# Two loads cut in two, and two value projections taken in turn, in a one-core attention-plus-MLP kernel

## The chip, the core and the metric

The kernel runs on one core of a Trainium2 chip. The core has a matrix engine (TensorE, PE in the profile, with its weight loads as PEld), a vector engine (VectorE, DVE), a scalar engine (ScalarE, ACT), a general one (GpSimd, POOL) and SyncE (SP), which here only issues transfers (DMAs). The metric is the device time of one execution in microseconds (us); lower is better. The time before is 173.61 us, the median of three runs (173.14, 173.61 and 174.13).

## The reference

```python
def reference(A_x, A_wqkv, A_w_phi, A_wo, B_x, B_w1, B_b1, B_w2):
    def _A_ref(x, wqkv, w_phi, wo):
        B, S, D = x.shape
        H = 32; Dh = D // H
        qkv = (lambda x, *d: x.transpose(*d))((x @ wqkv).reshape(B, S, 3, H, Dh), 2, 0, 3, 1, 4)
        q, k, v = qkv[0], qkv[1], qkv[2]
        pq = jnp.einsum("bhsd,hdf->bhsf", q, w_phi)
        pk = jnp.einsum("bhsd,hdf->bhsf", k, w_phi)
        phi_q = jnp.concatenate([_softmax(pq, axis=-1), _softmax(-pq, axis=-1)], axis=-1)
        phi_k = jnp.concatenate([_softmax(pk, axis=-1), _softmax(-pk, axis=-1)], axis=-1)
        kv = jnp.einsum("bhsf,bhsd->bhfd", phi_k, v)
        z  = jnp.einsum("bhsf->bhf", phi_k)
        num = jnp.einsum("bhqf,bhfd->bhqd", phi_q, kv)
        den = jnp.einsum("bhqf,bhf->bhq", phi_q, z)[..., None] + 1e-6
        o = num / den
        return (lambda x, *d: x.transpose(*d))(o, 0, 2, 1, 3).reshape(B, S, D) @ wo

    def _B_ref(x, w1, b1, w2):
        h = jnp.einsum("bsd,df->bsf", x, w1) + b1
        sp = jnp.log1p(jnp.exp(-jnp.abs(h))) + jnp.where(h > 0, h, jnp.zeros_like(h))
        act = h * jnp.tanh(sp)
        return jnp.einsum("bsf,fd->bsd", act, w2)

    x = A_x
    xn = _layernorm(x, axis=-1)
    return x + _A_ref(xn, A_wqkv, A_w_phi, A_wo) + _B_ref(xn, B_w1, B_b1, B_w2)
```

There are S = 2048 tokens of D = 512 numbers, 32 heads of 16 and F = 1792 hidden units, in bf16. A layer norm feeds two branches: an attention without a softmax over tokens (each head's 16 key or query features become 32 by two softmaxes) and a two-layer network with the Mish activation. Their sum is added to x.

## The kernel before

The tokens are cut into 16 tiles of 128 and four groups of four tiles. A tile of x is loaded with its tokens on the 128 partitions (`x_sb`), its mean and variance are taken on VectorE (line 165 and 167), it is normalised there (line 176) into `xn`, and it is turned so that the 512 features lie on the partitions in four blocks (`xnT`). For the first four tiles TensorE turns the tile by an identity (line 609) and VectorE or ScalarE copies the result (line 627); for the others a transposing DMA does it (line 181).

From `xnT` TensorE makes the keys' and queries' logits (`pl`, line 229, or 244 for the first two tiles), the values (`pv`, line 229) and the hidden units (`ph`, line 263). Each such product is a sum over the four feature blocks: four matmuls of 128x512 into one PSUM bank, with `xnT` as the weights for logits and values, and with the first-layer weights `w_sb` as the weights and four tiles of `xnT` streamed for hidden units. So a hidden unit needs all four tiles of a group, while values and logits need one tile. The values' weights are `wv`, four blocks of 128 rows by 512, in one tile of SBUF.

The order of all work is written out by hand in `STEPS`, a list of short names that are run one after the other; each engine takes its instructions in that order and waits on semaphores where data or a buffer isn't ready. The names that matter here, with the number of the tile, and after an `@` the PSUM bank:

- `LS t`: mean and variance of tile t, on VectorE. `RS t`: its inverse root, on ScalarE (`a`) or GpSimd (`p`). `AZ t`: the normalising, on VectorE.
- `TP t`: turning tile t on TensorE. `TC t`: the copy into `xnT`, by VectorE (`v`) or ScalarE (`a`).
- `F0`, `FD`: the keys' weights multiplied by w_phi, block by block, and their copies into `wkp`. The last of these copies on VectorE stands just ahead of `LS 2`.
- `LP i`: the logits of tiles 0 and 1, both tiles in turn for each feature block. `L 0 t`: the logits of tile t of group 0; `LC 0 t`: their copy.
- `V t`: the values of tile t. `VC t`: their copy, on ScalarE (`a`) or VectorE (`v`).
- `H u`: hidden unit block u, with 14 to a group; `H 6` is the first to run. `M u`: its activation on ScalarE.
- `LN`, `AP`: the norm of a later group; `WL`, `E`: logits and softmaxes.

In the stretch around the change the list reads: LP i; RS 2; LC 0 1; V 1; LS 3; AZ 2; RS 3; AZ 3; TP 2; V 0; TC 2; LC 0 0; TP 3; L 0 2; VC 1; TC 3; LC 0 2; H 6; L 0 3; VC 0.

The loads at the start are issued on SP, one behind the other in one queue: tile 0, tile 1, two blocks of the keys' weights, a transposing load of the rest (`wT`), tiles 2 and 3 together, `wv`, the first half of w1 (columns of hidden blocks 0 to 6), tiles 4 to 7, the rest of w1, tiles 8 to 11. ScalarE issues two small ones, the biases and w_phi (`wsrc`). The transfers of SP and ScalarE take eight semaphores in turn, and an issue first waits until the transfer eight before it has landed.

```python
    for t in range(2):
        nc.sync.dma_start(x_sb[:, t, :], x_v[:, t, :])
...
    nc.sync.dma_start(x_sb[:, 2:4, :], x_v[:, 2:4, :])
    nc.sync.dma_start(wv[:], wqkv_v[:, :, 2 * D : 3 * D])
    nc.sync.dma_start(w1_sb[:, :, 0 : 7 * P], w1_v[:, :, 0 : 7 * P])
    nc.sync.dma_start(x_sb[:, 4:8, :], x_v[:, 4:8, :])
```

Of the kernel before, what the change touches and what calls it, by code (L numbers as in the profile page):

```python
# [23 lines left out]
AW 256; AW 512; AW 128; AW 512; AW 256; AW 256; AW 512; AW 256; LS 0; AW 512; AW 512; LS 1; AW 256;  # L24
AW 256; AW 64; AW 128; RS 0 a; AW 512; PB @1; CB; AW 512; TW 0 @3; AZ 0; RS 1 a; AZ 1; TW 1 @0; TP 0
@2; TP 1 @5; TK 0 a; TC 0 a; WB v; TK 1 v; F0 0 @4; F0 1 @0; TC 1 v; F0 2 @2; FD 0 a; FD 2 a; FD 1
v; LS 2; F0 3 @1; FD 3 a; LP i @5,3; RS 2 a; LC 0 1 a; V 1 @1; LS 3; AZ 2; RS 3 p; AZ 3; TP 2 @0; V
0 @2; TC 2 v; LC 0 0 a; TP 3 @4; L 0 2 @5; VC 1 a; TC 3 a; LC 0 2 a; H 6 @4; L 0 3 @0; VC 0 v; LN 1;
LC 0 3 a; H 0 @1; H 1 @0; E 0 0; DX 2; AP 1 0; H 2 @5; AP 1 1; H 9 @2; M 2; H 3 @3; DX 3; M 1; M 9;
H 4 @5; M 0; M 6; H 10 @2; M 4; H 8 @1; KM; H 5 @5; H 11 @4; M 3; LN 2; M 8; E 0 1; M 5; H 7 @3; H  # L30
12 @5; M 10; AP 2 0; WL 1; M 11; H 17 @4; M 7; AM; L 1 0 @0; WL 2; L 1 3 @3; M 12; X 0 1; AP 2 1; X
# [31 lines left out]
def kernel(  # L63
# [12 lines left out]
    nc = tc.nc  # L76
    P = 128
    S, D, NH, DH, F = 2048, 512, 32, 16, 1792
# [3 lines left out]
    KT = D // P  # L82
# [4 lines left out]
    x_v = A_x.flatten_outer_dims().rearrange("(t p) d -> p t d", p=P)  # L87
    o_v = out.flatten_outer_dims().rearrange("(t p) d -> p t d", p=P)
    wqkv_v = A_wqkv.rearrange("(kt p) c -> p kt c", p=P)
# [17 lines left out]
    x_sb = persist.tile([P, NT, D], BF16, name="x_sb")  # L107
    xnT = persist.tile([P, NT, KT, P], BF16, name="xnT")
# [4 lines left out]
    wv = wts.tile([P, KT, D], BF16, name="wv")  # L113
# [27 lines left out]
    def bank(b, name, dtype=FP32):  # L141

        return ps.tile([P, 512], dtype, name=name, tag=f"bank{b}")
# [82 lines left out]
    def project(w, t, pp):  # L226

        for kt in range(KT):
            nc.tensor.matmul(  # L229
                pp, lhsT=xnT[:, t, kt, :], rhs=w(kt),  # L230
                start=(kt == 0), stop=(kt == KT - 1),
            )
        return pp

    pv_of, ph_of, pl_of = {}, {}, {}
# [12 lines left out]

    def value(t, b):
        pv_of[t] = project(values, t, bank(b, "pv")[:])  # L250

    def keep(t, copy):
        copy(
            vext[t // TPG % 2][:, t % TPG, :, 0:64],
            pv_of.pop(t).rearrange("p (j c) -> p j c", j=8),
        )
# [27 lines left out]
    def take(s, i, copy):  # L284
        if s not in p_of:
            p_of[s] = smx.tile([P, TPG, 512], BF16, name="p_sb")
        copy(p_of[s][:, i, :], pl_of.pop((s, i)))  # L287
# [238 lines left out]
    nc.scalar.dma_start(b1b[:], b1_v[:, :])  # L526
    with nc.allow_non_contiguous_dma(reason="tiny w_phi load"):
        nc.scalar.dma_start(wsrc[:], wphi_v)
    nc.sync.dma_start(x_sb[:, 2:4, :], x_v[:, 2:4, :])  # L529
    nc.sync.dma_start(wv[:], wqkv_v[:, :, 2 * D : 3 * D])  # L530
    nc.sync.dma_start(w1_sb[:, :, 0 : 7 * P], w1_v[:, :, 0 : 7 * P])
    nc.sync.dma_start(x_sb[:, 4:8, :], x_v[:, 4:8, :])
    nc.sync.dma_start(w1_sb[:, :, 7 * P : F], w1_v[:, :, 7 * P : F])
# [128 lines left out]
    def load_queries():  # L662
# [9 lines left out]
        "F0": lambda kt, b: fold(wT_of[0], kt, b), "FD": lambda kt, c: unfold(wkp, kt, copies[c]),  # L672
        "LN": stats, "AP": apply, "DX": load_tokens, "DW": load_weights, "WL": wide,
        "L": logits, "LC": lambda s, i, c: take(s, i, copies[c]),
        "V": value, "VC": lambda t, c: keep(t, copies[c]),
        "H": hidden, "M": mish,
        "E": extremes, "X": exponentials, "S": sums,
# [42 lines left out]
```

## Time and profile before

| | |
|---|---|
| median of three runs | 173.61 us |
| the profiled execution's own time | 174.09 us |
| its span in the profile | 172.3 us |
| TensorE busy | 168.1 us, 98% |
| VectorE busy | 141.8 us, 82% |
| ScalarE busy | 124.9 us, 72% |
| DMA engines' share, 8.6 to 12.9 us of the span | 9 tenths or more |
| granted TensorE clock | 0.999 |

Times in the trace count from the start of the span. A row of the timeline gives start, duration, engine, line, operation, and what is written from what; in brackets stands the engine's idle time before it and what ended it. A row of the chain gives start, duration and what the end of the run waited for. A row of a stretch gives its length, then for each engine its busy time and number of instructions (TensorE, weight loads, VectorE, ScalarE, GpSimd), the clock, the DMA engines' share and GB/s. A row of the DMA view gives the tile, the issuing engine, the number of issues, the size and the time from issue to landing. Matmuls overlap their neighbours, so four of them take less than the end of the last minus the start of the first.

### The profile page before, as it was taken

The numbers are of one execution on the slowest core, as the hardware profiler recorded it, in microseconds if no ns is written. First come the engines' busy times: TensorE is split into PE (matmuls) and PEld (weight loads), VectorE is DVE, ScalarE is ACT, GpSimd is POOL, SyncE is SP. The second block draws the span as 40 slices with busy tenths as digits, with TensorE's granted clock in tenths as the row PEclk, the third lists the DMA queues.
The fourth block names the chain that finished last, engine by engine and source line by source line (L and its number), as shares of the span: only waits on it lengthen the run. The fifth ranks groups of instructions, "written<-read, shape, count | busy, mean of one in ns | idle before, by whom it ended". The sixth has DMA issues, their size and how long they took to land.

```text
span 172.3 us, 2749 instructions
## 1 busy us (share of the span) xinstructions
PE 168.1 (98%) x1051; PEld 82.4 (48%) x1051; DVE 141.8 (82%) x220; ACT 124.9 (72%) x204; POOL 7.4 (4%) x21
## 2 busy tenths in 40 slices
PE   8989999999999999999999999999999999999993
PEld 3644444444444554454445644544444444554452
DVE  3677999989999999439989999799799998884333
ACT  3765989998999999789978989977282792432200
POOL 4021230200000000000000000000000000000000
PEclk9999999999999999999999999999999999999999
DMA  4997094276099200000000194309235628778641
GB/s 128 298 374 244 3 213 103 48 139 108 17 199 360 95 4 0 0 0 4 0 0 0 34 114 100 61 7 162 80 100 113 152 56 194 151 162 208 90 125 61
DMA packets 46297, 18.55 MB, mean 108 GB/s; under 512 B 38092, under 2 KB 46284, under 8 KB 46284
## 3 DMA queue, kind: packets, MB, share of 16 engines
q1 hardware_dynamic: 45584, 18.26, 44.7%
q10 hardware_dynamic: 700, 0.12, 0.4%
q8 instruction: 8, 0.13, 0.3%
q14 instruction: 5, 0.04, 0.1%
HBM read 7.10 MB, written 2.10 MB: 53 GB/s over the span
## 4 chain that ended last, share of the span: by engine, by line
PE 93%; DMA 3%; SPq 2%; issue 0%; DVE 0%
PE ph L263 28%; PE po L497 28%; PE pl L229 14%; PE pv L229 8%; PE po L504 8%; DMA wv<-in_A_wqkv_dram 3%; PE pnd L452 2%; PE pkv L421 2%; PE pwide L229 1%; SPq L523 1%; SPq L518 0%; SPq L529 0%; PE ptr L609 0%; SPq L522 0%; PE pfold L203 0%
## 5 line engine op out<-in xcount | busy, mean ns | idle before, releaser
L497 PE MATMUL po<-w_sb,acts 128*128 128x512 bf16 (+2 forms) x238 | 50.8, 366 | 0.0
L263 PE MATMUL ph<-xnT,w_sb 128*128 128x512 bf16 x224 | 50.3, 379 | 0.0
L274 ACT ACTIVATE acts<-ph,b1f 128x512 bf16<-128x512 f32 x56 | 35.8, 698 | 3.1 <-PE ph L263 3.0
L340 DVE TENSOR_REDUCE s<-e 128x128 f32<-128x2048 bf16 x16 | 36.3, 2276 | 0.5 <-ACT e L323 0.5
L263 PEld LDWEIGHTS <-w_sb 128*128 128x128 bf16 x224 | 21.6, 98 | 25.8 <-issue 0.2
L497 PEld LDWEIGHTS <-acts 128*128 128x128 bf16 x238 | 22.1, 98 | 23.6
L323 ACT ACTIVATE e<-e 128x2048 bf16<-128x2048 bf16 x16 | 30.4, 1915 | 0.0
L229 PEld LDWEIGHTS <-xnT 128*128 128x128 bf16 x184 | 17.5, 98 | 21.3 <-DMA wv<-in_A_wqkv_dram 1.1
L287 ACT CAST p_sb<-pl 128x512 bf16<-128x512 f32 x26 | 14.8, 589 | 4.8 <-PE pl L229 4.8
L511 DVE TENSOR_TENSOR x_sb<-po,x_sb 128x512 bf16<-128x512 f32 (+2 forms) x17 | 11.0, 657 | 8.3 <-PE po L504 8.3
L229 PE MATMUL pv<-wv,xnT 128*128 128x512 bf16 x64 | 15.4, 379 | 0.6 <-DMA wv<-in_A_wqkv_dram 0.6
L504 PE MATMUL po<-wqk,xnT 128*128 128x512 bf16 (+2 forms) x68 | 15.6, 366 | 0.0
L229 PE MATMUL pl<-wqk,xnT 128*128 128x512 bf16 x64 | 15.6, 379 | 0.0
L467 ACT COPY ds<-pnd 128x32 f32<-128x32 f32 x16 | 2.9, 183 | 16.5 <-PE pnd L452 16.5
L307 DVE TENSOR_TENSOR e<-p_sb,m 128x2048 bf16<-128x2048 bf16 x8 | 9.8, 1225 | 5.4 <-PE pkv L421 5.1
L165 DVE BATCH_NORM_STATS2 stats<-x_sb 128x6 f32<-128x512 bf16 x16 | 10.1, 680 | 4.6 <-DMA x_sb<-in_A_x_dram 4.6
L139 ACT ACT_TABLE_LOAD x10 | 12.8, 1283 | 0.2
L298 DVE TENSOR_TENSOR m<-m 128x512 bf16<-128x512 bf16 (+1 forms) x32 | 11.5, 359 | 1.1
L229 PE MATMUL pl<-wkp,xnT 128*128 128x512 bf16 x48 | 12.0, 379 | 0.0
L298 DVE TENSOR_TENSOR m<-p_sb 128x1024 bf16<-128x1024 bf16 x16 | 10.9, 682 | 0.5 <-ACT p_sb L287 0.5
L307 DVE TENSOR_TENSOR e<-m,p_sb 128x2048 bf16<-128x2048 bf16 x8 | 9.8, 1226 | 0.3
L374 DVE TENSOR_TENSOR e<-e,r 128x2048 bf16<-128x2048 bf16 x8 | 9.6, 1218 | 0.5 <-ACT r L349 0.5
(72 smaller groups left out, 130.3 us busy)
## 6 DMA issues: line engine op xcount, KB each, us to landing
w_sb<-in_B_w_dram SPq DMA_DIRECT2D x4, 896.0 KB, 8.4
out_dram<-x_sb SPq DMA_DIRECT2D x15, 128.0 KB, 2.0
x_sb<-in_A_x_dram SPq DMA_DIRECT2D x3, 512.0 KB, 8.6
wv<-in_A_wqkv_dram SPq DMA_DIRECT2D x1, 512.0 KB, 5.7
wqk<-in_A_wo_dram SPq DMA_DIRECT2D x1, 512.0 KB, 4.3
x_sb<-in_A_x_dram SPq DMA_DIRECT2D x2, 128.0 KB, 2.1
wkp<-in_A_wqkv_dram SPq DMA_DIRECT2D x1, 256.0 KB, 3.4
x_sb<-in_A_x_dram SPq DMA_DIRECT2D x1, 256.0 KB, 4.9
```

Source lines behind the costliest of these rows:

```text
L139: nc.scalar.preload_act_table_set(name)
L229: nc.tensor.matmul(pp, lhsT=xnT[:, t, kt, :], rhs=w(kt), start=(kt == 0), stop=(kt == KT - 1),)
L263: nc.tensor.matmul(ph_of[u][:], lhsT=w1_sb[:, kt, f * P : (f + 1) * P], rhs=xnT[:, g * TPG : (g + 1) * TPG, kt, :], start=(kt == 0), stop= ...
L274: nc.scalar.activation(acts[:, f, g * 512 : (g + 1) * 512], ph_of.pop(u)[:], ACT.Mish, bias=b1f[:, f : f + 1])
L287: copy(p_of[s][:, i, :], pl_of.pop((s, i)))
L298: nc.vector.tensor_tensor(out=m[:], in0=src[:, :, 0:half], in1=src[:, :, half : 2 * half], op=op)
L307: nc.vector.tensor_tensor(out=e_of[s][:].rearrange("p t j l c -> p (t j) l c")[:, :, pl, :].rearrange("p t (c e o) -> p t c e o", e=8, o=2 ...
L323: nc.scalar.activation(v, v, ACT.Exp)
L340: nc.vector.reduce_sum(t[:], pair(s, k).rearrange("p t j l (c e) -> p (t j l c) e", e=16), axis=AX.X)
L497: nc.tensor.matmul(po_of[t, c.stop][:, c], lhsT=acts[:, f, t * P : (t + 1) * P], rhs=w2_sb[:, f, c], start=(f == 0), stop=False,)
L504: nc.tensor.matmul(po_of[t, c.stop][:, c], lhsT=oT_of[t // 2][:, t % 2 * 4 + j, :], rhs=wo_sb[:, j, c], start=False, stop=(j == 3),)
L511: nc.vector.tensor_tensor(out=y, in0=po_of.pop((t, c.stop))[:, c], in1=y, op=ALU.add)
```

## The change

```diff
@@ STEPS @@
-v; LS 2; F0 3 @1; FD 3 a; LP i @5,3; RS 2 a; LC 0 1 a; V 1 @1; LS 3; AZ 2; RS 3 p; AZ 3; TP 2 @0; V
-0 @2; TC 2 v; LC 0 0 a; TP 3 @4; L 0 2 @5; VC 1 a; TC 3 a; LC 0 2 a; H 6 @4; L 0 3 @0; VC 0 v; LN 1;
+v; LS 2; F0 3 @1; FD 3 a; LP i @5,3; RS 2 a; LC 0 1 a; VA @1,2; LS 3; AZ 2; RS 3 p; AZ 3; TP 2 @0;
+VB; TC 2 v; LC 0 0 a; TP 3 @4; L 0 2 @5; VC 1 a; TC 3 a; LC 0 2 a; H 6 @4; L 0 3 @0; VC 0 v; LN 1;
@@ new function @@
+    def first_values(h, *b):
+
+        if h == 0:
+            for t, i in zip((1, 0), b):
+                pv_of[t] = bank(i, "pv")[:]
+        k = (2 * h, 2 * h + 1)
+        pairs = [(t, kt) for kt in k for t in (1, 0)] if h == 0 else [(t, kt) for t in (1, 0) for kt in k]
+        for t, kt in pairs:
+            nc.tensor.matmul(
+                pv_of[t], lhsT=xnT[:, t, kt, :], rhs=wv[:, kt, :],
+                start=(kt == 0), stop=(kt == KT - 1),
+            )
@@ loads @@
-    nc.sync.dma_start(x_sb[:, 2:4, :], x_v[:, 2:4, :])
-    nc.sync.dma_start(wv[:], wqkv_v[:, :, 2 * D : 3 * D])
+    for t in range(2, 4):
+        nc.sync.dma_start(x_sb[:, t, :], x_v[:, t, :])
+    for kt in (slice(0, 2), slice(2, 4)):
+        nc.sync.dma_start(wv[:, kt, :], wqkv_v[:, kt, 2 * D : 3 * D])
@@ names @@
+        "VA": lambda *b: first_values(0, *b), "VB": lambda: first_values(1),
```

Tiles 2 and 3 of x come by a transfer each, and `wv` by two transfers, of two row blocks each (half 0 and half 1). In place of V 1, TensorE runs VA: the first two feature blocks of the values of tiles 1 and 0, in turn, into two banks. In place of V 0 it runs VB: the other two blocks, first tile 1's, then tile 0's.

On TensorE, between the last matmul of LP and the turn of tile 3, the kernel before has these rows (`pv_230` is the bank of tile 1's values, `pv_246` that of tile 0's; `DMAHW7` is the semaphore of wv's transfer):

```order
L229 LDWEIGHTS xnT_86 [waits DMAHW7_49]
L229 MATMUL pv_230<-wv_91,xnT_86 128x512 [waits PE_49]
L229 LDWEIGHTS xnT_86
L229 MATMUL pv_230<-wv_91,xnT_86 128x512
...
L609 LDWEIGHTS xn_135 [waits DVE_49]
L609 MATMUL ptr_241<-ident_98,xn_135 128x128
...
L229 LDWEIGHTS xnT_86
L229 MATMUL pv_246<-wv_91,xnT_86 128x512
```

And the changed kernel has these at the same place (`pv_232` is tile 1's bank, `pv_233` tile 0's; `DMAHW0` and `DMAHW1` are the semaphores of the halves):

```order
L260 LDWEIGHTS xnT_86 [waits DMAHW0_49]
L260 MATMUL pv_232<-wv_91,xnT_86 128x512 [waits PE_49]
L260 LDWEIGHTS xnT_86
L260 MATMUL pv_233<-wv_91,xnT_86 128x512
...
L624 LDWEIGHTS xn_137 [waits DVE_49]
L624 MATMUL ptr_244<-ident_98,xn_137 128x128
...
L260 LDWEIGHTS xnT_86
L260 MATMUL pv_232<-wv_91,xnT_86 128x512 [waits DMAHW1_49]
```

The number and kind of TensorE's instructions are the same; the one wait for all of wv became a wait for each half, with the turn of tile 2 between them.

On SP the kernel before issues, after the transposing load of the keys' weights:

```order
L529 DMA x_sb<-in_A_x_dram 128x2x512
L530 DMA wv<-in_A_wqkv_dram 128x4x512
L531 DMA w_sb<-in_B_w_dram 128x4x896 [waits DMAHW0_49]
L532 DMA x_sb<-in_A_x_dram 128x4x512 [waits DMAHW1_49]
L533 DMA w_sb<-in_B_w_dram 128x4x896 [waits DMAHW2_49]
```

And the changed kernel:

```order
L543 DMA x_sb<-in_A_x_dram 128x512 x2
L545 DMA wv<-in_A_wqkv_dram 128x2x512 [waits DMAHW0_49]
L545 DMA wv<-in_A_wqkv_dram 128x2x512 [waits DMAHW1_49]
L546 DMA w_sb<-in_B_w_dram 128x4x896 [waits DMAHW2_49]
L547 DMA x_sb<-in_A_x_dram 128x4x512 [waits DMAHW3_49]
L548 DMA w_sb<-in_B_w_dram 128x4x896 [waits DMAHW4_49]
```

Every load behind the four stands two issues later in the queue, and each takes the semaphore two further on: the first half of w1 took that of the biases (`DMAHW0`) and takes that of w_phi (`DMAHW2`).

## The prediction

> **What bounds the kernel now.** I read the page first: its busy line and the head of its chain of waits.
>
> ```profile
> PE 168.1 (98%) x1051; PEld 82.4 (48%) x1051; DVE 141.8 (82%) x220; ACT 124.9 (72%) x204; POOL 7.4 (4%) x21
> PE 93%; DMA 3%; SPq 2%; issue 0%; DVE 0%
> ```
>
> TensorE is the kernel. The only thing beside it that weighs on the chain is one DMA. Next, the same chain in order of time:
>
> ```profile
> 4.19 5.69 DMA wv<-in_A_wqkv_dram
> 9.88 0.05 issue
> 9.93 1.04 PE pv L229 x4
> 10.96 0.22 PE ptr L609 x4
> 11.19 0.86 PE pv L229 x4
> ...
> 169.33 0.24 PE po L504 x4
> ```
>
> The values' weights land at 9.88 us and from 9.93 on TensorE runs without a break to 169.57. So only what makes the work after 9.93 start earlier, or opens a gap in it, can change the time. The views by stretch and by single matmuls give the size of the hole:
>
> ```profile
> 9.35:9.93 0.58, 0.01 (x1) 0.01 (x1) 0.58 (x2) 0.49 (x3) 0.00 (x0) 1.00 1.07 403
> 9.93:12.97 3.04, 3.04 (x20) 1.63 (x21) 1.94 (x6) 2.14 (x5) 0.88 (x2) 1.00 1.07 373
> 8.96 0.38 PE L244 MATMUL pl<-wkp,xnT 128*128 128x512 bf16 x1
> PE pv L229 <- DMA wv<-in_A_wqkv_dram: 0.6, 1, 0.6
> ```
>
> 0.58 us stand empty by the modelled ends. Four matmuls of this shape take 0.86 in the unbroken chain, 0.216 apart, so the one after 8.96 could have begun at 9.18: the most that can be won here is 9.93 - 9.18 = 0.75 us, 0.43% of the run.
>
> **What stands just behind the hole.** The timeline of the same stretch shows a second chain, of VectorE, that is nearly as late:
>
> ```profile
> 7.14 0.69 DVE L160 CAST wkp<-pfold 128x512 bf16<-128x512 f32 x1 [0.16 <-PE pfold L151]
> 8.46 0.69 DVE L165 BATCH_NORM_STATS2 stats<-x_sb 128x6 f32<-128x512 bf16 x1 [0.62 <-DMA x_sb<-in_A_x_dram]
> 10.08 0.38 DVE L176 TENSOR_SCALAR xn<-x_sb,mv,rstd 128x512 bf16<-128x512 bf16 x1
> 10.58 0.42 PEld L609 LDWEIGHTS <-xn 128*128 128x128 bf16 x4
> 11.00 0.59 ACT L253 CAST vext<-pv 128x512 bf16<-128x512 f32 x1
> 11.25 0.41 DVE L176 TENSOR_SCALAR xn<-x_sb,mv,rstd 128x512 bf16<-128x512 bf16 x1 [0.79 <-POOL rstd L172]
> 11.58 0.42 DVE L627 COPY xnT<-ptr 128x512 bf16<-128x512 bf16 x1
> 11.72 0.38 PEld L609 LDWEIGHTS <-xn 128*128 128x128 bf16 x4 [0.16 <-DVE xn L176]
> 12.11 1.03 PE L229 MATMUL pl<-wkp,xnT 128*128 128x512 bf16 x4
> 12.31 0.59 ACT L627 COPY xnT<-ptr 128x512 bf16<-128x512 bf16 x1 [0.72 <-PE ptr L609]
> 12.97 1.03 PE L263 MATMUL ph<-xnT,w_sb 128*128 128x512 bf16 x4
> ```
>
> Tile 2's statistics wait for the pair transfer until 8.46. From there the chain has no slack: tile 2 normalised at 10.46, turned from 10.58; tile 3 normalised at 11.66 and turned from 11.72; tile 2's copy done at 12.00, its logits (L 0 2) from 12.11. ScalarE's copy of tile 3 ends at 12.90 and the first hidden unit (H 6) follows at 12.97. TensorE is therefore fed by two chains that meet within 0.1 us: moving only one would move nothing.
>
> **The change, transfer by transfer.** The view of the DMAs, with the issues of the timeline:
>
> ```profile
> x_sb<-in_A_x_dram SPq DMA_DIRECT2D x1, 256.0 KB, 4.9
> wv<-in_A_wqkv_dram SPq DMA_DIRECT2D x1, 512.0 KB, 5.7
> x_sb<-in_A_x_dram SPq DMA_DIRECT2D x1, 512.0 KB, 8.6
> w_sb<-in_B_w_dram SPq DMA_DIRECT2D x1, 896.0 KB, 10.4
> x_sb<-in_A_x_dram SPq DMA_DIRECT2D x1, 128.0 KB, 2.1
> x_sb<-in_A_x_dram SPq DMA_DIRECT2D x1, 128.0 KB, 2.2
> 0.79 0.87 SPq L518 DMA_DIRECT2D x_sb<-in_A_x_dram  x2
> 1.71 0.43 SPq L522 DMA_DIRECT2D wkp<-in_A_wqkv_dram  x1
> 3.56 0.57 SPq L529 DMA_DIRECT2D x_sb<-in_A_x_dram  x1
> 4.19 0.46 SPq L530 DMA_DIRECT2D wv<-in_A_wqkv_dram  x1
> 4.70 0.51 SPq L531 DMA_DIRECT2D w_sb<-in_B_w_dram  x1
> 5.24 0.51 SPq L532 DMA_DIRECT2D x_sb<-in_A_x_dram  x1
> ```
>
> Landings are issue plus the last column: the pair 8.46, wv 9.88, tiles 4 to 7 at 13.88. Between 8.46 and 9.88 lie 512 KB, 360 KB/us; between 9.88 and 13.88 lie 896 + 512 KB, 352 KB/us. The transfers stream one behind the other. By that rate I estimate the first half of w1 at 9.88 + 896/352 = 12.4.
>
> *Tiles 2 and 3 apart.* The bytes up to tile 2 are 128 KB fewer: 128/360 = 0.36, so tile 2 lands at 8.10 and tile 3 still at 8.46. VectorE is free from 7.83 (7.14 + 0.69), so its chain moves by 0.36; tile 3's statistics start at about 8.9, after its landing. Bounds: 0 if both halves of the old pair still finish together, and 8.46 - 7.83 = 0.63 if tile 2 is there when VectorE is free. I take 0.36; the first two tiles, issued about 0.43 apart, landed some 0.55 apart, which speaks for separate landings.
>
> *wv in halves.* Half 0 lands 256/360 = 0.71 before wv did: 9.17. Half 1 stays at 9.88. VA (four matmuls, both tiles, rows 0 and 1) then runs from 9.18 to 10.04 in place of V 1 from 9.93. The turn of tile 2 needs xn: 10.46 - 0.36 = 10.10, begins about 10.22 and takes 0.22. VB from 10.44, with half 1 there since 9.88 (0.56 to spare), to 11.30. Tile 3's xn: 11.66 - 0.36 = 11.30, turn from 11.36 to 11.58. L 0 2 must have tile 2's copy, 12.00 - 0.36 = 11.64: start 11.75 against 12.11. TensorE won 0.75 at VA and gave half of it back to VectorE's chain; the stall moves from wv to xn and xnT. H 6 comes at 12.97 - 0.36 = 12.61, and w1's first half (12.4) is just in time: this is the next thing late, and without the VectorE chain it alone would allow only about 0.4.
>
> *Edits costed at nothing.* VA and VB issue the same eight matmuls and weight loads as V 1 and V 0. VC 1 can start later, since V 1's sum now ends in VB (10.44 + 0.22 + 0.38 = 11.04 against the 11.00 shown); ScalarE idles 0.72 before the copy of tile 3, which covers it; without the cover it would cost 0.04. The two added issues on SP: two tiles at 0.41 + 0.05 and two halves at the 0.43 of a two-row-block transfer + 0.05 end 0.76 later than now, so w1's first half is issued at 5.46 and the tiles 4 to 7 at 6.00. Cover: the queue ahead of w1 is not through until 9.88, and a transfer that found an almost empty queue landed 2.1 after its issue, so 9.88 - 5.46 - 2.1 = 2.3 us remain; without cover the 0.76 would land on w1 and on tiles 4 to 7 whole. The issue of w1 also waits now for w_phi's transfer instead of the biases':
>
> ```profile
> wsrc<-in_A_w_phi_dram ACTq DMA_DIRECT2D x1, 16.0 KB, 3.7
> 1.48 0.41 ACTq L528 DMA_DIRECT2D wsrc<-in_A_w_phi_dram  x1
> ```
>
> It landed at 5.2, before 5.46: no wait, with 0.26 to spare. Behind it on SP stand tiles 4 to 7, the rest of w1 and tiles 8 to 11.
>
> *Does 0.36 survive?* Tiles 4 to 7 land at 13.88 as before, so VectorE from there on does not move while TensorE does. The margins:
>
> ```profile
> 20.25 2.63 SPq L181 DMA_TRANSPOSE xnT<-xn  x2
> xnT<-xn SPq DMA_TRANSPOSE x4, 3.3
> 25.92 1.03 PE L263 MATMUL ph<-xnT,w_sb 128*128 128x512 bf16 x4
> 37.33 0.69 DVE L298 TENSOR_TENSOR m<-p_sb 128x1024 bf16<-128x1024 bf16 x1 [0.48 <-ACT p_sb L287]
> ```
>
> The second turn of tiles 4 to 7 is issued about 21.6 and lands about 24.9; its user stands at 25.92: 1.0 to spare. The rest of w1 lands at 5.79 + 10.4 = 16.2, its first user (H 9) stands five groups of 0.86 after H 6's 12.97, at 17.3: 1.1. VectorE itself waits 0.48 for ScalarE at 37.33, so it can be that much later against TensorE before anything is lost. All exceed 0.36, and from there VectorE follows ScalarE and ScalarE TensorE. Sum: -0.36 + 0 + 0 = -0.36. The profiled execution took 174.09 with a span of 172.3; it would take 173.73 with 171.9. That execution is 0.48 above the median of the runs shown, 173.61. I carry the same 0.36 over: 173.25.
>
> **Rivals.**
> A: *more is won.* Tile 2 is there by 7.83 and w1's first half lands ahead of 12.4. For it: the 256 KB pair took 4.9 us where the rate asks for 0.7, so a part of it may have been ready long before. Against: w1 stands behind the same bytes. Then 0.63 to 0.75 is won: about 172.9, and 172.7 with a lucky landing of all.
> B: *nothing is won.* The landing of tile 2 does not come earlier, VectorE's chain holds TensorE as now, and VA's early start ends in a longer wait before the turn of tile 2. Or the executions near the median hardly wait for wv at all: the runs spread from 173.14 to 174.13 and the profiled one is among the longest. 173.6.
> C: *slower, by the start of each transfer.* If a transfer holds the queue for a time c before its bytes flow, the two added ones put 2c on half 1, w1 and tiles 4 to 7. From wv after the pair, c is 0. From the pair: wT, the transfer ahead of it,
>
> ```profile
> 2.18 1.33 SPq L523 DMA_TRANSPOSE wT<-in_A_wqkv_dram  x1
> wT<-in_A_wqkv_dram SPq DMA_TRANSPOSE x1, 3.9
> ```
>
> landed at 6.1, the pair 2.4 later for 0.7 us of bytes: c up to 1.6. It decides from c = 0.3, where w1 lands at 12.4 + 0.6 and H 6 is no earlier than now. At the middle, c = 0.8: w1 at 14.0, H 6 at about 14.1, 1.1 late: 174.7. At c = 0.67 the loss passes 0.87. The Trainium skill speaks for it: "DMA: Bandwidth & Descriptors" (section "Rules for kernel authors") would coalesce many small transfers into one large one, and its section on the anatomy of one DMA gives a fixed part of about 2.0 us each; taken as serial that would be 4 us more, about 177 by an estimate from that page. The trace disagrees with the serial reading, since wv landed 1.42 after the pair with 512 KB in between.
>
> **Chances.** Forecast 0.56, A 0.13, B 0.15, C 0.16. What a measurement of this kernel can tell from no change is about 0.5%, 0.87 us: below 172.74 or above 174.48. The forecast's own range, 172.9 to 173.6, lies inside, but the spread of the executions may carry 0.08 of it below; with 0.08 from A and 0.01 from B, faster is 0.17. Slower is 0.13 from C and 0.01 from B, 0.14. The rest, 0.69, is no change. The range takes A's end and C to its middle: 172.5 to 174.7.
>
> **What would show it.** Right: the wait of the pv matmuls for wv gone or under 0.1; VA at about 9.2; tile 2's statistics at about 8.1; small waits of TensorE for xn and xnT between 10 and 12; H 6 at 12.6; everything behind it 0.3 to 0.4 earlier to the end. Wrong: tile 2's statistics still at 8.4 or later (B); a new wait of VB for half 1, of H 6 for w1, or the statistics of tile 4 later than 14.2 (C); an SP wait ahead of w1's issue; or a gap in TensorE after 13 us that gives the 0.36 back.

## The result and the profile after

The changed kernel is a little slower. Over 22 runs of each its median is 174.21 us (173.42 to 174.99) against 173.59 (173.10 to 174.17); the ratio is 1.0032, with an interval of 1.0018 to 1.0047 (the ratios here and below differ a little from the quotients of the medians). By the ratio that is 0.56 us: inside the 0.5% that the prediction called the bound of what can be told, but clear of 1 with this many runs. Forecast was 173.25, a gain of 0.36.

The page of the changed kernel, its busy line and the head of its chain of waits:

```profile
PE 167.3 (97%) x1036; PEld 82.3 (48%) x1051; DVE 141.6 (82%) x220; ACT 125.0 (72%) x204; POOL 7.4 (4%) x21
PE 90%; DMA 4%; SPq 3%; issue 1%; DVE 0%
```

TensorE is still the kernel (its count is 15 lower because records are missing), but the chain gives 4% to a DMA where it gave 3%, and 3% to SP's issues where it gave 2%. The chain in order of time says which DMA (start, duration, what the end of the run waited for):

```profile
5.64 7.32 DMA w_sb<-in_B_w_dram
...
13.01 1.04 PE ph L276 x4
14.04 0.86 PE pl L229 x4
14.91 10.36 PE ph L276 x48
```

Before, the chain passed through wv, which landed at 9.88. Now it passes through the first half of w1, which lands at 5.64 + 7.32 = 12.96; the first hidden unit, H 6, starts at 13.01. The timeline of the changed kernel, TensorE, VectorE and SP's issues, shows both ends of what happened (start, duration, engine, line, operation; idle time before in brackets):

```profile
3.55 1.05 SPq L543 DMA_DIRECT2D x_sb<-in_A_x_dram  x2
4.64 0.95 SPq L545 DMA_DIRECT2D wv<-in_A_wqkv_dram  x2
5.64 0.47 SPq L546 DMA_DIRECT2D w_sb<-in_B_w_dram  x1
6.15 0.51 SPq L547 DMA_DIRECT2D x_sb<-in_A_x_dram  x1
7.78 0.69 DVE L165 BATCH_NORM_STATS2 stats<-x_sb 128x6 f32<-128x512 bf16 x1
9.21 1.03 PE L260 MATMUL pv<-wv,xnT 128*128 128x512 bf16 x4
10.29 1.03 PE L260 MATMUL pv<-wv,xnT 128*128 128x512 bf16 x4
11.38 1.03 PE L229 MATMUL pl<-wkp,xnT 128*128 128x512 bf16 x4
13.01 1.04 PE L276 MATMUL ph<-xnT,w_sb 128*128 128x512 bf16 x4 [0.60 <-DMA w_sb<-in_B_w_dram]
14.39 2.47 DVE L165 BATCH_NORM_STATS2 stats<-x_sb 128x6 f32<-128x512 bf16 x4 [2.34 <-DMA x_sb<-in_A_x_dram]
```

The front did what the change says: tile 2's statistics wait for nothing, VA starts at 9.21, VB runs at 10.29, the logits L 0 2 at 11.38 in place of 12.11. TensorE would be ready for H 6 at 11.38 + 0.86 = 12.24. Then it stands still until w1 is there, 0.77 later, and H 6 begins where it began before (12.97).

The DMA view of the changed kernel, of the issues between 3 and 7 us, and of the two issues behind wv taken alone (size, time from issue to landing):

```profile
wv<-in_A_wqkv_dram SPq DMA_DIRECT2D x2, 256.0 KB, 3.6
x_sb<-in_A_x_dram SPq DMA_DIRECT2D x2, 128.0 KB, 2.9
w_sb<-in_B_w_dram SPq DMA_DIRECT2D x1, 896.0 KB, 7.3
x_sb<-in_A_x_dram SPq DMA_DIRECT2D x1, 512.0 KB, 8.2
```

Tiles 4 to 7 land at 6.15 + 8.2 = 14.35 instead of 13.88. The same stretch by throughput, 6 to 12 us (busy time and count of TensorE, weight loads, VectorE, ScalarE, GpSimd; clock; DMA share; GB/s), before:

```profile
6.00:12.00 6.00, 5.42 (x46) 2.99 (x44) 4.36 (x11) 4.48 (x10) 0.88 (x2) 1.00 1.05 354
```

and after:

```profile
6.00:12.00 6.00, 5.92 (x49) 3.46 (x48) 4.93 (x13) 5.04 (x11) 0.88 (x2) 1.00 0.97 309
```

The DMA engines count as busy nearly throughout in both (shares of 1.05 and 0.97), yet they move 45 GB/s less: 45 x 6 = 270 KB fewer in these 6 us, and at 354 KB/us that is 0.76 us of loading.

Why is a kernel whose H 6 starts at 13.01 slower by 0.56 than one whose H 6 starts at 12.97? Because the profiled execution of the kernel before was not its usual one. In sixteen profiled executions of this study (all but e4, which moves H 6), the time minus the start of the first hidden unit is the same:

| kernel | first hidden unit starts | time of that execution | difference |
|---|---|---|---|
| before, first profile | 12.97 | 174.09 | 161.12 |
| before, second profile (e10) | 12.05 | 173.17 | 161.12 |
| after, first profile | 13.01 | 174.23 | 161.22 |
| after, second profile (e11) | 12.79 | 174.03 | 161.24 |
| the twelve others | 12.20 to 13.45 | 173.42 to 174.69 | 161.06 to 161.25 |

So the time is settled when the first hidden unit starts. By that sum the median of the kernel before stands for a start at 173.59 - 161.12 = 12.47, and the median of the changed one for 174.21 - 161.23 = 12.98. The question for the experiments is what puts it there.

### The profile page after: what moved, and what is told of

Read it like the earlier page. It is cut to its first block, busy times and chain, and to the rows that moved or that the text cites. A ratio compares the mean times of both kernels' runs of the same rounds, so it can differ in the third digit from the quotient of the medians.

```text
span 172.5 us, 2736 instructions
## 1 busy us (share of the span) xinstructions
PE 167.3 (97%) x1036; PEld 82.3 (48%) x1051; DVE 141.6 (82%) x220; ACT 125.0 (72%) x204; POOL 7.4 (4%) x21
## 4 chain that ended last, share of the span: by engine, by line
PE 90%; DMA 4%; SPq 3%; issue 1%; DVE 0%
PE ph L276 28%; PE po L510 28%; PE pl L229 13%; PE po L517 8%; PE pv L229 7%; DMA w_sb<-in_B_w_dram 4%; PE pnd L465 2%; PE pkv L434 2%; PE pwide L229 1%; SPq L536 1%; SPq L543 1%; SPq L545 1%; SPq L531 0%; SPq L535 0%; PE pfold L203 0%
## 5 line engine op out<-in xcount | busy, mean ns | idle before, releaser
L510 PE MATMUL po<-w_sb,acts 128*128 128x512 bf16 (+2 forms) x232 | 50.2, 366 | 0.3
L229 PEld LDWEIGHTS <-xnT 128*128 128x128 bf16 x176 | 16.9, 98 | 19.7 <-issue 0.2
L517 PE MATMUL po<-wqk,xnT 128*128 128x512 bf16 (+2 forms) x65 | 15.0, 366 | 0.2
L229 PE MATMUL pv<-wv,xnT 128*128 128x512 bf16 x55 | 13.3, 379 | 0.1
L311 DVE TENSOR_TENSOR m<-p_sb 128x1024 bf16<-128x1024 bf16 x16 | 10.9, 680 | 0.0
```

The costliest lines, as they stand in the source:

```text
L229: nc.tensor.matmul(pp, lhsT=xnT[:, t, kt, :], rhs=w(kt), start=(kt == 0), stop=(kt == KT - 1),)
L311: nc.vector.tensor_tensor(out=m[:], in0=src[:, :, 0:half], in1=src[:, :, half : 2 * half], op=op)
L510: nc.tensor.matmul(po_of[t, c.stop][:, c], lhsT=acts[:, f, t * P : (t + 1) * P], rhs=w2_sb[:, f, c], start=(f == 0), stop=False,)
L517: nc.tensor.matmul(po_of[t, c.stop][:, c], lhsT=oT_of[t // 2][:, t % 2 * 4 + j, :], rhs=wo_sb[:, j, c], start=False, stop=(j == 3),)
```

## The experiments

Theory S (rival C of the prediction, at a small price): each transfer put ahead in the queue delays all that stands behind it, whatever its size. Its rivals: the later issue of w1 (5.64 instead of 4.70) is what counts; the order VA, VB costs something; the cutting of the data itself does. Medians of the kernel before beside the runs were 173.69 (e1 to e4), 173.76 (e5 to e8), 173.67 (e9 to e12) and 173.66 (e13 to e15).

**The parts of the change, one at a time**

e1, on the kernel before:

```diff
-    nc.sync.dma_start(x_sb[:, 2:4, :], x_v[:, 2:4, :])
+    for t in range(2, 4):
+        nc.sync.dma_start(x_sb[:, t, :], x_v[:, t, :])
```

> Only tiles 2 and 3 get a transfer each; wv whole, V 1 and V 0 as before. Late-landing theory (each added transfer brings w1's first half and tiles 4 to 7 later, 0.6 and 0.5 us for two of them in the changed kernel's profile): one added transfer, so about half of that: w1's first half at 12.6 to 12.7, tiles 4 to 7 at 14.1, the wait for wv still there, time 0.2 to 0.4 above before. Order theory (VA and VB themselves cost): no change, within 0.1 of before. Chance theory (the added transfers cost nothing, the profile's landings only scatter): within 0.1 of before or below it.

e2, on the changed kernel:

```diff
-    for t in range(2, 4):
-        nc.sync.dma_start(x_sb[:, t, :], x_v[:, t, :])
+    nc.sync.dma_start(x_sb[:, 2:4, :], x_v[:, 2:4, :])
```

> Only wv in halves with VA and VB; tiles 2 and 3 together. Late-landing theory: 0.2 to 0.4 above before, w1's first half at 12.6 to 12.7, H 6 waiting for it. Order theory: as slow as the changed kernel, 0.5 to 0.6 above before. Chance theory: 0.1 to 0.3 below before, since VA starts earlier.

e3, the changed order on the loads of the kernel before:

```diff
-RS 2 a; LC 0 1 a; V 1 @1; LS 3; AZ 2; RS 3 p; AZ 3; TP 2 @0; V 0 @2;
+RS 2 a; LC 0 1 a; VA @1,2; LS 3; AZ 2; RS 3 p; AZ 3; TP 2 @0; VB;
```

> VA and VB in place of V 1 and V 0, but wv in one transfer and tiles 2 and 3 in one: the loads of before. Late-landing theory: no change, within 0.15 of before, w1's first half at about 12.4 and tiles 4 to 7 at about 13.9. Order theory: 0.5 to 0.6 above before.

Measured: e1 173.82, ratio 1.000 [0.998, 1.002]; e2 173.83, 1.0020 [1.0005, 1.0034]; e3 173.88, 1.0009 [0.9992, 1.0026]. None gains. For one added transfer nothing shows in e1 and 0.05 to 0.34% in e2; for the order alone nothing shows. In e3, with wv uncut, no matmul waited for wv; VA started at 9.46 because the engine itself was not free earlier. In e1 TensorE waited 0.83 for wv. GB/s from 6 to 12 us: 327, 342 and, with uncut loads, 350.

**Filling the wait for w1**

e4, on the changed kernel:

```diff
-LC 0 2 a; H 6 @4; L 0 3 @0; VC 0 v; LN 1;
+LC 0 2 a; L 0 3 @0; H 6 @4; VC 0 v; LN 1;
```

> The changed kernel with the logits of tile 3 (L 0 3) ahead of the first hidden unit (H 6), so that TensorE has 0.86 us of work that needs no w1 while w1's first half is on the way. Late-landing theory with H 6's wait as what costs: the wait of 0.6 for w1 goes, H 6 at about 13.1 with L 0 3 done, 0.6 below the changed kernel, at or below before. Late-landing theory with the tiles 4 to 7 as what costs (VectorE's chain behind them): TensorE's gain is given back later, within 0.2 of the changed kernel. Order theory: within 0.2 of the changed kernel.

Measured: 174.03, 1.0026 [1.0011, 1.0042], not told apart from the change. The timeline of e4, TensorE:

```profile
13.46 3.62 PE L276 MATMUL ph<-xnT,w_sb 128*128 128x512 bf16 x16
17.27 7.94 PE L276 MATMUL ph<-xnT,w_sb 128*128 128x512 bf16 x36 [0.19 <-DMA w_sb<-in_B_w_dram]
...
29.36 5.53 PE L276 MATMUL ph<-xnT,w_sb 128*128 128x512 bf16 x24
```

The wait at H 6 is gone, although w1's first half landed only at 5.63 + 7.8 = 13.43 here: TensorE starts H 0 at 13.46 + 0.86 = 14.32 in place of 14.74. But now H 9 stops at 17.27 for the rest of w1 (issued at 6.69, landed 17.22), and the 24 matmuls from 29.36 take 5.53 where the changed kernel's row of 24 from 29.42 takes 5.34, while ScalarE's activations there start at 33.13 instead of 32.80. So in this execution, whose first half of w1 came later than in any other, the wait at H 6 was only the first place at which late loads show; closing it handed the lateness to the next load and to ScalarE. How much of that holds for its median, one execution can't tell.

**Later issue without added transfers**

e5, on the kernel before (the three loads are taken from their place behind wv into `LW`, which runs behind `RS 1`; its copy makes SP wait until ScalarE is there; the word that it writes is loaded over):

```diff
+    def load_late():
+        nc.scalar.copy(w1_sb[:, 0, 0:1], b1f[:, 0:1])
+        nc.sync.dma_start(w1_sb[:, :, 0 : 7 * P], w1_v[:, :, 0 : 7 * P])
+        nc.sync.dma_start(x_sb[:, 4:8, :], x_v[:, 4:8, :])
+        nc.sync.dma_start(w1_sb[:, :, 7 * P : F], w1_v[:, :, 7 * P : F])
```

> The loads of before, uncut, but w1's first half, tiles 4 to 7 and the rest of w1 are issued only after a one-column ScalarE copy into w1's buffer that ends at about 5.6 us, so about 0.9 us later than before and at the same time as in the changed kernel; no transfer is added. Issue theory (what delays the landings is that SP gets to these loads 0.94 us later): w1's first half and tiles 4 to 7 land about 0.5 later, time 0.4 to 0.6 above before. Transfer theory (each added transfer costs the queue some time, whenever it is issued): no change, within 0.15 of before.

e15, the same edit a second time, beside e14:

> The late issue of w1 and tiles 4 to 7 without an added transfer, a second time, since its first interval reached from -0.05% to 0.32%. Issue theory: 0.4 to 0.6 above before, first half of w1 at 12.8 or later. Transfer theory: within 0.2 of before, rate near 345.

Measured: 173.89, 1.0014 [0.9995, 1.0032], and 173.76, 1.0000 [0.9980, 1.0020]. With w1 issued at 5.67 and 5.68, as late as in the changed kernel, H 6 started at 12.51 and 12.74, both times in an unbroken row behind TensorE's own work. The prediction's cover for the later issue holds: it is not what costs. (e15 moved only 322 GB/s from 6 to 12 us, and no time was lost by it: the throughput of this window is a hint and not a measure of the time.)

**More transfers, and transfers without a cut**

e6, on the changed kernel:

```diff
-    for kt in (slice(0, 2), slice(2, 4)):
+    for kt in range(KT):
```

> The changed kernel with wv in four transfers, one a row block: four transfers added to before instead of two, and the issue of w1 another 0.9 us later. Transfer theory: the loss doubles, w1's first half about 0.5 later than in the changed kernel, time 1.0 to 1.3 above before. Issue theory: also later, by as much or more. If neither holds (the loss comes from the order of VA and VB, or from chance), the time stays within 0.2 of the changed kernel.

Measured: 174.87, 1.0057 [1.0035, 1.0080]: by the ratios four added transfers cost nearly twice what two cost, though the interval overlaps with that of the change, 1.0018 to 1.0047. The timeline of e6 (issue of w1, then H 6):

```profile
6.55 0.43 SPq L546 DMA_DIRECT2D w_sb<-in_B_w_dram  x1
13.24 1.04 PE L276 MATMUL ph<-xnT,w_sb 128*128 128x512 bf16 x4 [0.58 <-DMA w_sb<-in_B_w_dram]
```

It is the same wait, later; the throughput is 292 GB/s.

e9, on the kernel before, two transfers of 8 KB that nobody uses, one ahead of wv and one behind it:

```diff
     nc.sync.dma_start(x_sb[:, 2:4, :], x_v[:, 2:4, :])
+    nc.sync.dma_start(more[:, 0, :], x_v[:, 2, 0:32])
     nc.sync.dma_start(wv[:], wqkv_v[:, :, 2 * D : 3 * D])
+    nc.sync.dma_start(more[:, 1, :], x_v[:, 3, 0:32])
```

> The loads of before, uncut, and two more transfers of 8 KB each into a buffer that nothing reads, one behind the pair of tiles and one behind wv, in the places of the queue where the change adds its own. Transfer theory (the number of transfers costs, not the bytes or the cut): w1's first half, tiles 4 to 7 and the rest of w1 land 0.4 to 0.9 later than with the uncut loads, the rate between 6 and 12 us falls from about 350 to about 310 GB/s, time 0.4 to 0.7 above before. Cut theory (it is the cutting of wv and the pair, not the count): within 0.2 of before, rate about 345.

Measured: 174.11, 1.0031 [1.0014, 1.0048], what the change costs, with no load cut and VA, VB absent. e9's chain, which was one of its milder executions (173.83):

```profile
4.69 4.80 DMA wv<-in_A_wqkv_dram
9.49 0.04 issue
9.53 1.04 PE pv L229 x4
```

and its throughput from 6 to 12 us:

```profile
6.00:12.00 6.00, 5.86 (x50) 3.26 (x47) 4.62 (x13) 4.72 (x11) 0.88 (x2) 1.00 0.98 312
```

The rate is 312, as with the two cuts (309). But the DMA view of e9 shows no late landing behind it:

```profile
w_sb<-in_B_w_dram SPq DMA_DIRECT2D x1, 896.0 KB, 6.2
x_sb<-in_A_x_dram SPq DMA_DIRECT2D x1, 512.0 KB, 6.9
```

The first half of w1 landed at 5.71 + 6.2 = 11.91 and tiles 4 to 7 at 6.19 + 6.9 = 13.09, the latter earlier than in the first profile of the kernel before (13.88, at 354 GB/s). So the rate alone says little about when a load lands. The chain runs over wv, and H 6 follows at 12.58 without a wait; where the median execution of e9 loses its 0.54 us isn't seen in this one. Its added transfers also consist of rows of 64 bytes; whether two with longer rows, uncut, cost the same was not tried.

e14, on the kernel before, the same two small transfers behind the rest of w1:

```diff
     nc.sync.dma_start(w1_sb[:, :, 7 * P : F], w1_v[:, :, 7 * P : F])
+    for t in range(2):
+        nc.sync.dma_start(more[:, t, :], x_v[:, 2 + t, 0:32])
```

> The loads of before and the two 8 KB transfers, but both behind the rest of w1 in the queue, so that nothing that is needed early stands behind them. Serial theory (an added transfer delays what stands behind it in the queue): within 0.15 of before, rate between 6 and 12 us near 350. Crowding theory (the number of transfers that are queued at once slows them all): as slow as with the two small ones ahead, 0.4 or more above before, rate near 310.

Measured: 173.80, 1.0003 [0.9983, 1.0024]. Behind the loads that matter no cost shows. The intervals of e9 and e14 still overlap between 1.0014 and 1.0024, so that the place decides is likely rather than proven.

**The same kernels again**

e10 is the kernel before, unchanged:

> The kernel before, unchanged, for a second profile of it. If the wait for wv of its first profile is the rule, it stands here too, at 0.5 or more, and wv lands near 9.9. If that was one slow landing, as the three other profiles with the uncut early loads suggest (wv at 8.6 to 9.4, no wait), there is no wait here, wv at 8.6 to 9.4, H 6 at about 12.5. Time within 0.1 of before.

Measured: 173.31, 0.9989 [0.9969, 1.0009]; the profiled execution took 173.17. Its chain:

```profile
1.73 3.37 DMA wkp<-in_A_wqkv_dram
...
7.31 1.87 PE pl L244 x8
9.17 0.86 PE pv L229 x4
10.04 0.22 PE ptr L609 x4
10.26 0.86 PE pv L229 x4
11.12 0.22 PE ptr L609 x4
11.35 0.86 PE pl L229 x4
12.21 0.86 PE ph L263 x4
```

and its DMA view, issues between 3 and 7 us:

```profile
wv<-in_A_wqkv_dram SPq DMA_DIRECT2D x1, 512.0 KB, 4.7
```

wv landed at 4.19 + 4.7 = 8.9, ahead of TensorE, and the wait that the change was to shorten was not there at all: matmul after matmul from the keys' weights to the hidden units. Tiles 4 to 7 landed at 5.24 + 7.5 = 12.7, where the first profile had 13.88. Nothing in the program differs.

e11 is the changed kernel, unchanged:

> The changed kernel, unchanged, for a second profile. If the slow landings of its first profile are the rule: w1's first half at 12.8 or later, H 6 waiting for it, tiles 4 to 7 at 14.2 or later, the rate between 6 and 12 us near 300 GB/s; time 0.4 to 0.7 above before. If they were chance: w1's first half at 12.4 or earlier.

Measured: 174.04, 1.0029 [1.0013, 1.0046]; the profiled execution took 174.03. Its timeline:

```profile
8.86 1.03 PE L260 MATMUL pv<-wv,xnT 128*128 128x512 bf16 x4
...
11.03 1.03 PE L229 MATMUL pl<-wkp,xnT 128*128 128x512 bf16 x4
12.79 1.04 PE L276 MATMUL ph<-xnT,w_sb 128*128 128x512 bf16 x4 [0.73 <-DMA w_sb<-in_B_w_dram]
...
14.28 2.47 DVE L165 BATCH_NORM_STATS2 stats<-x_sb 128x6 f32<-128x512 bf16 x4 [2.58 <-DMA x_sb<-in_A_x_dram]
```

The wait for w1 is there again, in full: TensorE was ready at 11.03 + 0.86 = 11.89. VA began 0.35 earlier than in the first profile and only 0.22 of it came through to H 6.

The traces also hold each landing in parts: 16 updates of the transfer's semaphore, of which the last is the landing that the views show. In the first profile of the kernel before, 15 parts of the pair of tiles had landed by 6.99 and the last at 8.44; 15 parts of wv had landed by 8.55 and the last at 9.88. The wait that the change was to shorten hung on one part of sixteen. Of the eight profiles with the pair and wv whole and nothing added ahead of them (before, e3, e5, e8, e10, e13, e14, e15), only this one and that of e14 (0.40) wait for wv. In the other six wv was there by 8.56 to 9.37, and TensorE itself came to the values between 9.01 and 9.70.

Read in the same way, the first half of w1 shows where nobody waits for it, too. With the early loads uncut its last part lands between 11.27 and 12.45 (before, e3, e5, e10, e14, e15; 11.97 on average), with one transfer added at 12.26 and 12.28 (e1, e2), with both cuts between 12.75 and 13.41 (both profiles of the change, e4, e12; 13.09 on average), with four added transfers at 13.20 (e6). So w1 lands later in each profile with both cuts than in any uncut one. Half of its parts are there by 10.8 to 11.2 without the cuts and by 10.9 to 11.6 with both, so most of the delay is in the last parts. What holds these back isn't shown.

**The loads alone, and what H 6 needs**

e12, the changed kernel's loads with the order of the kernel before:

```diff
-RS 2 a; LC 0 1 a; VA @1,2; LS 3; AZ 2; RS 3 p; AZ 3; TP 2 @0; VB;
+RS 2 a; LC 0 1 a; V 1 @1; LS 3; AZ 2; RS 3 p; AZ 3; TP 2 @0; V 0 @2;
```

> The loads of the changed kernel, both cut, with V 1 and V 0 as before. If the loads set the time and the order of VA and VB is worth nothing: 0.4 to 0.7 above before, like the changed kernel, H 6 at 12.8 or later. If VA and VB cost something by themselves: nearer to before.

Measured: 174.42, 1.0047 [1.0027, 1.0067]. Its timeline shows V 1 cut by a wait for half 1, which landed at 10.8:

```profile
9.62 0.59 PE L229 MATMUL pv<-wv,xnT 128*128 128x512 bf16 x2
10.85 0.59 PE L229 MATMUL pv<-wv,xnT 128*128 128x512 bf16 x2 [0.63 <-DMA wv<-in_A_wqkv_dram]
```

The loads carry the loss. In this execution it comes in at wv: w1's first half landed at 5.63 + 7.6 = 13.23, and H 6, unbroken at 13.45, did not wait for it. VA and VB may win some of it back by bridging a late second half; the intervals of e12 and the change overlap.

e7, the changed kernel with w1 cut at block 5 instead of 7, the hidden units 3 and 6, and 4 and 9, changing places in the order so that the first half is enough; and e8, the same on the kernel before:

```diff
-    nc.sync.dma_start(w1_sb[:, :, 0 : 7 * P], w1_v[:, :, 0 : 7 * P])
+    nc.sync.dma_start(w1_sb[:, :, 0 : 5 * P], w1_v[:, :, 0 : 5 * P])
...
-    nc.sync.dma_start(w1_sb[:, :, 7 * P : F], w1_v[:, :, 7 * P : F])
+    nc.sync.dma_start(w1_sb[:, :, 5 * P : F], w1_v[:, :, 5 * P : F])
```

> The changed kernel with w1 cut behind hidden block 5 instead of 7 and the first hidden units taken in the order 3, 0, 1, 2, 4, so that 256 KB less lie ahead of the first hidden unit and of tiles 4 to 7. If the landings of w1's first part and of tiles 4 to 7 swallowed the gain: they come about 0.7 earlier than in the changed kernel, the wait ahead of the first hidden unit goes, time 0.6 to 0.8 below the changed kernel and 0.1 to 0.4 below before. If something else costs: within 0.2 of the changed kernel.

> The kernel before with the same cut of w1 and the same order of hidden units, none of the change. TensorE there waits for wv and not for w1, so the earlier landings should be worth nothing: within 0.15 of before. If it is 0.3 or more below before, the landing of tiles 4 to 7 or of w1 already set the time of the kernel before in most executions.

Measured: e7 173.89, 0.9998 [0.9984, 1.0012]; e8 173.50, 0.9985 [0.9966, 1.0004]. With 256 KB fewer ahead of it (640 KB, issued at 5.63, landed 6.5 later at 12.13) the first hidden unit of e7 starts at 12.20, and the loss of the change is gone: about 0.33% between e7 and the change, whose intervals do not touch. Together with the waits of H 6 in both profiles of the change and in e6, it puts the loss at w1's landing. With the smaller first half the change is level with the kernel before, and no better: e8, without the change, is at least as fast, so a part of the 0.33% (0.15% by e8, not clear of noise) may come from the smaller half alone. No version here beats the kernel before beyond its interval.

**The first two tiles**

e13, the reverse of e1 at the head of the queue, on the kernel before:

```diff
-    for t in range(2):
-        nc.sync.dma_start(x_sb[:, t, :], x_v[:, t, :])
+    nc.sync.dma_start(x_sb[:, 0:2, :], x_v[:, 0:2, :])
```

> The kernel before with tiles 0 and 1 in one transfer: one transfer fewer ahead of everything, the same bytes. Count theory (each transfer in the queue costs the stream about 20 GB/s of its rate between 6 and 12 us): rate at or above 356, w1's first half and tiles 4 to 7 no later than before, time 0.1 to 0.3 below before, unless tile 0's later landing (about 3.2 for 2.9) delays the head, which has some 0.5 to spare there. If the cost comes from cutting near the values' weights alone: within 0.15 of before.

Measured: 173.72, 1.0008 [0.9992, 1.0024]. The gain that theory S gives for one transfer fewer did not come. The loads behind were earlier (w1 issued at 4.30, landed 7.0 later at 11.3), but tile 0 came later with the pair, its statistics started at 3.74, TensorE got to V 1 only at 9.65, and H 6 at 12.69 was unbroken. The chain of e13 starts at the landing of the first tile and passes through none of the loads behind it; but TensorE came to V 1 as late in e15 (9.70), where these tiles are apart.

## Why the prediction was wrong

**Where TensorE waits: right for the profile shown.** VA was put at 9.18 and came at 9.21; the wait for wv went, and the stall moved. That proves little of the change, since V 1 of the unchanged kernel starts at 9.01 in e10. w1's first half was named as "the next thing late", and it was.

**Tiles 2 and 3 apart: the right way, for another reason.** Tile 2's statistics were put at 8.10, and started at 7.78 without a wait, the bound of 0.63 that belonged to rival A. The bytes were not what mattered: tile 2 landed at 3.55 + 2.9 = 6.45, where the count of bytes said 8.10, because the pair's 8.46 had been one late part. In e10 the whole pair landed at 3.56 + 3.8 = 7.36, so some of this gain comes without the change. L 0 2 came at 11.38 (11.75 was said), and TensorE was ready for H 6 at 12.24 (12.61 was said).

**"Edits costed at nothing": the step that failed.** It let two transfers more pass for 0 because the later issue is covered. The cover is real (e5, e15), but the issue is not the price. The price is in the queue: w1, put at 12.4, landed at 12.96 and 12.75; tiles 4 to 7, put "at 13.88 as before", at 14.35 and 14.24. This is rival C, whose price c I took as 0 in the forecast, "since wv landed 1.42 after the pair". That row was one landing in one execution, and landings scatter by more than c. (C's other row, the pair 2.4 behind wT, was the late part: 15 of 16 were there 0.9 behind wT.) Measured by e9, two transfers without any cut cost 0.31% of 173.67, 0.54 us, so 0.27 each, or 0.12 to 0.42 by the interval; C said that it decides from 0.3, and at 0.3 put w1 at 13.0 and H 6 "no earlier than now". That is nearly what the first profile shows. In the landings the delay is larger: w1's last part comes at 13.09 with both cuts and at 11.97 without, on average, 1.1 later for two. As a rough estimate, H 6 could have started at 12.47 by the median of the kernel before, so 13.09 - 12.47 = 0.6 of it reaches TensorE, near the 0.56 lost. I gave C 0.16 and priced it at c = 0.8.

The Trainium skill, "DMA: Bandwidth & Descriptors", section "Rules for kernel authors", would coalesce many small transfers into one large one, and the direction agrees here for pieces of 128 and 256 KB, at 1.0032 for the change. The same page's section "Anatomy of one DMA" gives a fixed part of about 2.0 us, fitted to transfers that GpSimd issues, while these are issued from SP; taken as serial it would be an estimate of 4 us for two, and e9 measured 0.54.

**"I carry the same 0.36 over": the second step that failed.** The working was made against an execution of 174.09 whose wv landed at 9.88, and moved to the median as it stood. The text noted in rival B that "the executions near the median hardly wait for wv at all", and e10 shows such a one; six of the eight profiles with these loads uncut do not wait for wv. Against H 6 at 12.97 the change loses nothing (13.01); against the 12.47 that the median implies it loses 0.5. By the two profiles, TensorE would be ready at 12.24 and 11.89, some 0.2 to 0.6 ahead of 12.47; waiting for w1 then takes 0.77 and 0.90. The difference, 0.5 and 0.3, is the loss.

**"Does 0.36 survive?": not reached.** The margins behind were never tested by the change, since nothing was won up to H 6. e4 tested them: 0.42 won at H 0, and given back at the rest of w1 (margin 1.1 by the prediction, gone because that load too came a microsecond later, 17.22 for 16.2) and by ScalarE near 33 us.

**What stays open.** Why an added transfer makes the last parts of a load behind it land later is not shown; the bytes (16 KB in e9), the later issue (e5, e15) and the order of the matmuls (e3) don't explain it. That e9's median execution loses its time at w1, as the change does, is inferred from its time alone: its one profile has w1 early. So the count of transfers, apart from the cutting, is likely the cause and not proven.

## What to carry to other kernels

Before a load is cut for the sake of a wait of half a microsecond, look at that wait in several executions: here it was absent in another one of the same program. The transfers added ahead of a full queue were paid for here at the load behind them with the least to spare, so look for that load, and put what is not urgent at the end. If a wait moves to the next load when filled, as in e4, look at all the loads; here fewer bytes ahead of the first user brought the time back (e7), while one transfer fewer at the head of the queue gained nothing (e13).

## What was not expected of the hardware

The landings of one and the same queue of loads scatter by about a microsecond between executions: wv at 8.9 and 9.9 and tiles 4 to 7 at 12.7 and 13.9 in two profiles of the kernel before. A landing is that of the last of 16 parts, and one part of wv came 1.3 us behind the other fifteen (8.55 and 9.88). Two transfers of 8 KB in front cost as much time as the cutting of two loads into pieces of 128 and 256 KB (1.0031 and 1.0032). And the time of a whole execution of 174 us can be read, to 0.2 us, from the start of one matmul at 13 us.
